# Splitting the first fetch of a block's tail values by segment, and moving three quarters of it to another queue

## The chip, the cores and the metric

The kernel runs on one core of a Trainium2 chip. The metric is the device time of one execution in microseconds (us), from three runs: the median is 1030.23 us, the lowest 1029.62 and the highest 1031.26. One further execution was recorded by the hardware profiler; all views quoted below come from that one.

The engines are named as in the profile: PE (TensorE matmuls), PEld (its weight loads), DVE (VectorE), ACT (ScalarE), POOL (GpSimd) and SP (SyncE, which here only issues transfers). A name with a q behind it (SPq, ACTq) is the engine's instruction queue when it issues a transfer. Transfers issued by SP and by ACT run on the same 16 DMA engines.

## What is computed

The program has two halves, each behind a layer norm with a residual: a recurrent attention with memory tokens (A), and a dense layer with a squared ReLU (B). Only A touches the change.

```python
for s in range(64):                     # 64 segments of 32 tokens
    xs = LN(x)[:, 32*s:32*s+32, :]      # [1, 32, 640]
    h = concat([mem, xs])               # 8 memory tokens + 32 tokens = 40
    q, k, v = h@Wq, h@Wk, h@Wv          # 32 heads of 128
    p = softmax(mask(q k^T / sqrt(128)))
    o = (p v) @ Wo                      # [1, 40, 640]
    mem = o[:, :8]                      # goes into the next segment
    out_A[32*s:32*s+32] = o[:, 8:]
h1 = x + out_A
out = h1 + (relu(LN(h1)@w1 + b1)**2) @ w2 + b2
```

The 64 segments are a chain: the memory of one is an input of the next. A query sees all memory and the tokens up to its own place; a memory query sees all 40 keys.

## The kernel before

**Blocks and steps.** Four segments make a block of 128 tokens; there are 16 blocks and 64 calls of `step(b, sp)`, block `b`, segment `sp`. Each step projects 32 rows: the 8 memory rows of this segment and its first 24 tokens. The last 8 tokens of each segment, its tail, cannot be among them, and since they do not depend on the memory they are projected ahead, for a whole block at a time (4 x 8 = 32 rows): `tail_units(b, "q" | "k" | "v")`. Queries and keys of the tails stay in SBUF. The values of the tails (`"v"`) need another layout, with the token on the partition axis within each of four groups of heads; they are written to DRAM (`vt_d`, line 279 in `tail_out`) and read back in that layout by `tails_v_in` (lines 331 to 336), four DMAs, one for each group of heads, into the tile `vt4` [128, 4 segments, 2, 128]. One such DMA moves 64 KB: 32 partitions, each 4 segments x 2 x 128 values of bf16, 2 KB that are contiguous in DRAM.

**Who reads it.** In step `sp` the four matmuls of line 452 (for each half of the heads) multiply the memory queries' weights by `vt4[r, sp, n, :]`, and one step later line 358 does the same for the tokens' queries. So a step reads only its own segment of the tile.

**The start.** Before the 64 steps, `start()` runs while the weights arrive. SP issues, in this order: rows of x, the five chunks of Wv (1 MB each, lines 117 to 120), one more piece of x, the five chunks of Wq, the five chunks of Wk, and Wo in six pieces (`load_wo`, lines 142 to 146; two of 1280 KB, four of 640 KB), then the x rows of blocks 1 and 2 (`load_x`). PE consumes the chunks as they land: `stream("v")`, `stream("q")` and `stream("k")` project block 0's first segment and its tails chunk by chunk, with the tail values of blocks 1 to 4 in between as filling. Block 0's tail values are stored by ACT's queue (line 282), and are fetched back by ACT's queue too: `tails_v_in(0, nc.scalar)` stands at line 709, behind `stream("q")`. Then comes step 0, which needs Wo at its end: `wo_rounds(main, pw, ...)`, lines 531 to 537. The order of Wo's pieces is that in which step 0 reads them; the last 14 of its 64 matmuls read the sixth piece.

**Order and waits.** The kernel is recorded under a manual schedule: each engine runs its instructions in the order in which the code calls them. Waits are added by the tile framework, which tracks the parts of tiles that an instruction reads and writes. Each DMA of the two queues takes the next of eight completion semaphores in turn, in program order, and a DMA that reuses a semaphore first waits until the DMA eight places before it has landed. So at most eight are in flight, and a queue can stand at a DMA that waits for one of the other queue. In the kernel as built, pieces 2, 4, 5 and 6 of Wo wait for the four DMAs of `tails_v_in(0)`.

**What stands behind on SP.** After the x rows of block 2, SP's next DMAs store tail values: three of blocks 5 and 6, whose rows are evacuated during step 0 into a ring of four `row` buffers (`rowtile`, line 217), then eight that had been parked elsewhere, then the four DMAs of `tails_v_in(1)`. Those three stores free `row` buffers that ACT's evacuations of step 1 write again (lines 224, 222 and 403).

Of the kernel before, what the change touches and what calls it, by code (L numbers as in the profile page):

```python
# [12 lines left out]
BF16 = mybir.dt.bfloat16  # L13
# [3 lines left out]
def kernel(  # L17
# [16 lines left out]
    nc = tc.nc  # L34
    _, S, D = A_x.shape
    _, H, E = A_Wq.shape
# [31 lines left out]
    s1 = ctx.enter_context(tc.tile_pool(name="s1", bufs=1))  # L68
    s2 = ctx.enter_context(tc.tile_pool(name="s2", bufs=2))
# [66 lines left out]
    for ch in range(2):  # L136
        nc.scalar.dma_start(out=o0[32 * ch:32 * ch + M, :].rearrange("m (c f) -> m c f", f=64),
                            in_=A_mem0[0].rearrange("m (c t f) -> t m c f", t=2, f=64)[ch])
# [25 lines left out]
    def ln_stats(b):  # L164
        xns[b] = stats(xts[b][:])

    def ln_norm(b):
        mv, rs = xns[b]
        xn = s1.tile([128, D], BF16, tag="xn", name="xn")
        xt = xts.pop(b)  # L170
        nc.vector.tensor_scalar(out=xn[:], in0=xt[:], scalar1=mv[:, 0:1], scalar2=rs[:, 0:1],
                                op0=ALU.subtract, op1=ALU.mult)
        xns[b] = xn

    def ln_transpose(b):

        xn = xns.pop(b)
        pt = mm.tile([128, 1024], BF16, tag="mm", name="pt")
        for c in range(DC):
            nc.tensor.transpose(out=pt[:, c * 128:(c + 1) * 128], in_=xn[:, c * 128:(c + 1) * 128], identity=ident[:])  # L180

        def out():
            if isinstance(b, tuple):
                hTt = s2.tile([128, DC, 4, TL, 4], BF16, tag="hTt", name="hTt")
                for c0, c1 in ((0, 2), (2, DC)):
                    nc.scalar.copy(out=hTt[:, c0:c1].rearrange("p c b k s -> p (c b) s k"),
                                   in_=pt[:, c0 * 128:c1 * 128].rearrange("p (a s k) -> p a s k", s=4, k=TL))
                hTts[b[1]] = hTt
                return
            hT4 = s2.tile([128, DC, 4, SEG], BF16, tag="hT4", name="hT4")  # L190
            ptv = pt[:, 0:640].rearrange("p (c s t) -> p c s t", c=DC, s=4)
            nc.scalar.copy(out=hT4[:, :, :, M:SEG], in_=ptv[:, :, :, 0:HD])
            hT4s[b] = hT4
        return out

    def proj(w, by, lhs, n, ps, c0, c1):

        if by == "columns":
            wr = w[:].rearrange("p (c g j n k e) -> p c n k g j e", c=DC, g=G, n=2, j=4, k=4)
        elif by == "half":  # L200
            wr = w[:].rearrange("p (c k j n e) -> p c n k j e", c=DC, k=G, n=2, j=4)
        else:
            wr = w[:].rearrange("p (c k n f) -> p c n k f", c=DC, k=G, n=2)
        for c in range(c0, c1):
            for k in range(4):
                nc.tensor.matmul(ps[32 * k:32 * k + 32, :], lhsT=lhs(c), rhs=wr[:, c, n, k], start=(c == 0), stop=(c == DC - 1))  # L206
# [10 lines left out]
    def rowtile():  # L217
        return s2.tile([128, 512], BF16, tag="row", name="row", bufs=4)

    def evac_row(which, row, ps):  # L220
        if which == "q":
            nc.scalar.mul(out=row, in_=ps, mul=scale)  # L222
        else:
            nc.scalar.copy(out=row, in_=ps)  # L224

    def flip(row, dst, n):
        nc.vector.transpose(out=dst[:, n * 16:(n + 1) * 16, 0:32], in_=row.rearrange("p (h e) -> p h e", e=32))  # L227
# [23 lines left out]
    def run(q, n):  # L251
        while n > 0 and q:
            q.pop(0)()
            n -= 1

    def tail_rows(b, c):
        return hTts[b // 4][:, c, b % 4].rearrange("p k s -> p (k s)")

    def tail_units(b, which):
        w = {"q": wq, "k": wk, "v": wv}[which]  # L260
        lhs = lambda c: tail_rows(b, c)
        st = {}

        def unit(n, c):
            def f():
                if c == 0:
                    st[n] = mmtile()
                proj(w, "columns" if which != "v" else "order", lhs, n, st[n], c, c + 1)
                if c == DC - 1:
                    tail_out(b, which, n, st[n][:])  # L270
            return f
        return [unit(n, c) for n in range(2) for c in range(DC)]

    def tail_out(b, which, n, ps):
        row = parked.pop(0) if which == "v" and 0 < b and parked else rowtile()[:]
        evac_row(which, row, ps)
        if which == "v":
            def store(eng=nc.sync):
                eng.dma_start(out=vt_d[b, 2 * n:2 * n + 2].rearrange("j r f -> r j f"),
                              in_=row.rearrange("r (j f) -> r j f", j=2))  # L280
            if b == 0:
                store(nc.scalar)
            elif b < 5:
                stores.append(store)
            else:
                store()
            return
        if n == 0:
            tails.setdefault(b, {})[which] = s2.tile([128, H, 32], BF16, tag=which + "Tt", name=which + "Tt")
        dst = tails[b][which]  # L290
        late.append(lambda: flip(row, dst, n))
# [28 lines left out]
    def tails_in(b, sp, which="qk", h0=0, h1=H):  # L320
        q, k = [tails[b][w][:].rearrange("p h (k s) -> p h s k", s=4)[:, h0:h1, sp, :] if w in which else None for w in "qk"]
        if "q" in which:
            nc.gpsimd.tensor_copy(out=qT[:, h0:h1, SEG:NK], in_=q)
        if "k" in which:
            nc.gpsimd.tensor_copy(out=kT[:, h0:h1, SEG:2 * SEG].rearrange("p h (j k) -> p h j k", k=TL),  # L325
                                  in_=k.unsqueeze(2).to_broadcast([128, h1 - h0, 4, TL]))

    vt4s, stores = {}, []
    vt_d = dram.tile([NB, 4, 128, 2 * E], BF16)

    def tails_v_in(b, eng):

        vt4s[b] = s2.tile([128, 4, 2, E], BF16, tag="vt4", name="vt4")
        src = vt_d[b].rearrange("j (g k s) f -> g j k (s f)", g=G, s=4)
        for g in range(G):
            eng.dma_start(out=vt4s[b][32 * g:32 * g + 32].rearrange("p s u e -> p (s u e)"), in_=src[g])

    def store_main(o, s):
        for ch in range(2):
# [38 lines left out]
    def step(b, sp, v=None):  # L378
# [8 lines left out]
        if sp == 1 and b + 1 < NB:  # L387
            tails_v_in(b + 1, nc.sync)
# [278 lines left out]
    def start():  # L667

        v = s2.tile([128, EG], BF16, tag="v", name="v")
        main = lambda c: hT4s[0][:, c, 0, :]  # L670
        units = []

        def stream(which, w, dst):
            pa = pop.tile([128, 4, 512], F32, tag="po", name="pa")
            for c in range(DC):
                for n in range(2):
                    proj(w, "half" if which == "v" else "columns", main, n, pa[:, n, :], c, c + 1)
                for n in range(2):
                    proj(w, "order" if which == "v" else "columns", lambda c: tail_rows(0, c), n, pa[:, 2 + n, :], c, c + 1)
                if c < DC - 1:  # L680
                    run(units, DC)
            for n in range(2):
                if which == "v":
                    nc.scalar.copy(out=v[:, n * 512:(n + 1) * 512], in_=pa[:, n, :])
                else:
                    row = rowtile()[:]
                    evac_row(which, row, pa[:, n, :])
                    flip(row, dst, n)
                    tail_out(0, which, n, pa[:, 2 + n, :])
                    run(late, 100)  # L690
                    tails_in(0, 0, which, n * 16, (n + 1) * 16)
            if which == "v":
                for n in range(2):
                    tail_out(0, which, n, pa[:, 2 + n, :])

        stream("v", wv, None)
        ln_stats(("t", 1))
        ln_norm(("t", 1))
        units += tail_units(1, "v")
        run(units, DC)  # L700
        ln_transpose(("t", 1))()
        run(units, DC)
        units += tail_units(2, "v") + tail_units(3, "v")
        stream("q", wq, qT)
        for n in range(2):
            spread(n)
        units += tail_units(4, "v")
        run(units, 2 * DC)
        tails_v_in(0, nc.scalar)
        units += tail_units(1, "q")  # L710
        stream("k", wk, kT)
        units += tail_units(1, "k")
        run(units, 2 * DC)
        run(late, 100)
        return v
# [11 lines left out]
    load_x(1)  # L727
    ln_transpose(("t", 0))()
    v0 = start()
    halves = [h for b in range(8, NB) for h in (tail_units(b, "v")[:DC], tail_units(b, "v")[DC:])]  # L730
    for b in range(NB):
        for sp in range(4):
# [40 lines left out]
            e = b * 4 + sp - (NS - 7)  # L773
# [30 lines left out]
    for t in range(S // NT):  # L804
# [32 lines left out]
        for q in range(NK4):  # L837
# [18 lines left out]
            for hh in range(2):  # L856
                b = t * NK4 + pr + 2 * hh
# [38 lines left out]
```

## Time and profile before

| | us |
|---|---|
| median of three runs | 1030.23 (1029.62 to 1031.26) |
| profiled execution, its own time | 1033.91 |
| its span, first to last instruction | 1031.8 |
| PE busy | 975.2 (95%) |
| DVE / ACT / POOL busy | 617.2 / 533.7 / 309.9 |
| mean granted TensorE clock | 0.993 |
| Wo's last piece lets PE go on (step 0) | 62.51 |
| PE begins step 1 | 65.49 |

PE is busy almost without a break from step 1 to the end; the start, up to some 65 us, is another stage, in which PE waits for weights. All places of the change lie in this stage or right behind it.

Rows of the timeline and of the chain give the start in us from the first instruction, the duration in us, and what ran; "x20" is the number of instructions merged into a row, and a bracket tells how long the engine had been idle before and what ended it. Rows of the window view give, for a stretch of time, each engine's busy time with its number of instructions, the granted TensorE clock (1.00 is full), the mean busy share of the 16 DMA engines and the bytes that they moved in GB/s. The view of DMA queues gives packets, megabytes and the share of 16 engines' time; q1 is SP's ring, q10 is ACT's, q8 and q14 carry instructions.

### The profile page before, as it was taken

To read this page: it belongs to the slowest core of one execution; us is meant where nothing else is said; L and a number is where in the kernel's file an instruction comes from. 1 tells how busy PE (TensorE), PEld (TensorE's weight loads), DVE (VectorE), ACT (ScalarE), POOL (GpSimd) and SP (SyncE) were. 2 spreads that over 40 slices of the span, in tenths; PEclk is the share of its full clock that TensorE was granted. 3 is DMA by queue.
4 is the path that set the end of the run, shared out by engine and by line. 5 is a ranking of instruction groups with operands and counts; after the bars stand their busy time and mean duration, and the time that the engine had idled before them with its cause. 6 is when DMAs were issued, how large, how long until landed. Compare 5 with 4: busy or idle time off the path is not lost.

```text
span 1031.8 us, 58965 instructions
## 1 busy us (share of the span) xinstructions
PE 975.2 (95%) x26960; PEld 578.7 (56%) x26960; DVE 617.2 (60%) x1740; ACT 533.7 (52%) x1229; POOL 309.9 (30%) x803
## 2 busy tenths in 40 slices
PE   6779899999999999999999999999999999999998
PEld 2345455655655555556655665555566565555565
DVE  2256566766666666666766666666665576566432
ACT  3335555555555555555555555555555555534431
POOL 1023333333333333333333232323333333343210
PEclk9989999999999999999999999999999999999999
DMA  9960101000101010000000000000000110612200
GB/s 361 381 195 21 23 7 31 7 25 6 35 7 29 7 37 12 23 14 25 16 21 16 15 27 14 22 14 27 15 21 9 47 34 7 195 59 68 77 26 26
DMA packets 38968, 51.57 MB, mean 50 GB/s; under 512 B 5952, under 2 KB 34752, under 8 KB 36800
## 3 DMA queue, kind: packets, MB, share of 16 engines
q1 hardware_dynamic: 37936, 47.29, 14.0%
q8 instruction: 210, 3.44, 1.4%
q10 hardware_dynamic: 784, 0.53, 0.2%
q14 instruction: 38, 0.31, 0.1%
HBM read 38.37 MB, written 9.44 MB: 46 GB/s over the span
## 4 chain that ended last, share of the span: by engine, by line
PE 88%; DMA 5%; issue 2%; DVE 2%; ACT 1%; SPq 1%; ACTq 0%; DVEq 0%; POOL 0%
PE ps L206 48%; PE pw L238 15%; PE y L847 6%; PE ps L815 5%; PE ps L238 3%; PE po L447 2%; PE po L353 2%; PE sm L419 2%; DMA vt_d<-row 1%; PE ps L491 1%; DMA wv<-in_A_Wv_dram 1%; DMA wo<-in_A_Wo_dram 1%; PE pm L316 1%; DMA vt<-vt_d 1%; DMA wq<-in_B_w_dram 1%
## 5 line engine op out<-in xcount | busy, mean ns | idle before, releaser
L206 PEld LDWEIGHTS <-hT 128*32 128x32 bf16 x7680 | 196.8, 97 | 179.9 <-issue 19.3
L238 PE MATMUL pw<-wo,oT 128*32 128x320 bf16 x4224 | 186.6, 301 | 9.3 <-issue 6.0
L206 PE MATMUL ps<-wv,hT 128*32 128x512 bf16 x2520 | 171.6, 379 | 2.6 <-issue 2.0
L206 PE MATMUL ps<-wq,hT 128*32 128x512 bf16 x2520 | 159.6, 381 | 5.3 <-DVE hT L318 5.3
L206 PE MATMUL ps<-wk,hT 128*32 128x512 bf16 x2520 | 159.2, 381 | 0.1
L238 PEld LDWEIGHTS <-oT 128*32 128x32 bf16 x4224 | 106.8, 96 | 62.3 <-issue 15.5
L222 ACT ACTIVATE row<-ps 128x512 bf16<-128x512 f32 x156 | 93.3, 599 | 74.8 <-PE ps L206 74.8
L227 DVE STREAM_TRANSPOSE qT<-row 128x512 bf16<-128x512 bf16 x128 | 90.3, 705 | 65.5 <-ACT row L222 65.4
L546 POOL TENSOR_TENSOR pkt<-ek,rk 128x64 bf16<-128x64 bf16 x64 | 19.0, 296 | 363.6 <-DVE rk L544 363.6
L224 ACT CAST row<-ps 128x512 bf16<-128x512 f32 x115 | 68.0, 591 | 32.9 <-PE ps L206 32.7
L325 POOL COPY kT<-kTt 128x1024 bf16<-128x1024 bf16 (+1 forms) x65 | 71.9, 1106 | 13.0 <-DVE kTt L227 13.0
L372 POOL COPY qz<-qT 128x96 bf16<-128x96 bf16 x126 | 33.6, 267 | 138.1 <-DVE qT L227 137.9
L206 PEld LDWEIGHTS <-hTt 128*32 128x32 bf16 x1920 | 54.1, 98 | 33.7 <-issue 4.5
L245 ACT COPY otmp<-pw 64x320 f32<-64x320 f32 x66 | 27.9, 422 | 83.2 <-PE pw L238 83.2
L246 DVE TENSOR_TENSOR o<-pw,otmp 64x320 bf16<-64x320 f32 x66 | 31.8, 482 | 63.2 <-ACT otmp L245 63.2
L363 ACT CAST oT<-po 128x512 bf16<-128x512 f32 x128 | 68.7, 589 | 1.6
L521 ACT CAST v<-ps 128x512 bf16<-128x512 f32 x63 | 36.9, 586 | 59.6 <-PE ps L206 59.6
L227 DVE STREAM_TRANSPOSE kT<-row 128x512 bf16<-128x512 bf16 x65 | 46.1, 709 | 32.1 <-ACT row L224 32.1
L542 DVE TENSOR_REDUCE zk<-ek 128x8 f32<-128x320 bf16 x64 | 31.1, 486 | 53.8 <-ACT ek L540 53.8
L847 PE MATMUL y<-wq,wk 128*128 128x320 bf16 x416 | 61.0, 299 | 0.2 <-DVE wk L824 0.2
L403 ACT CAST row<-ps 128x256 bf16<-128x256 f32 x126 | 40.8, 375 | 31.0 <-PE ps L206 29.9
L500 ACT CAST v<-ps 128x512 bf16<-128x512 f32 x63 | 36.9, 586 | 30.0 <-PE ps L206 30.0
(113 smaller groups left out, 1633.5 us busy)
## 6 DMA issues: line engine op xcount, KB each, us to landing
wv<-in_A_Wv_dram SPq DMA_DIRECT2D x5, 1024.0 KB
wq<-in_A_Wq_dram SPq DMA_DIRECT2D x5, 1024.0 KB
wk<-in_A_Wk_dram SPq DMA_DIRECT2D x5, 1024.0 KB
vt<-vt_d SPq DMA_DIRECT2D x60, 64.0 KB
xt<-in_A_x_dram SPq DMA_DIRECT2D x20, 160.0 KB
vt_d<-row SPq DMA_DIRECT2D x22, 128.0 KB
wo<-in_A_Wo_dram SPq DMA_DIRECT2D x2, 1280.0 KB
wo<-in_A_Wo_dram SPq DMA_DIRECT2D x4, 640.0 KB
```

What stands on the lines that cost most here:

```text
L206: nc.tensor.matmul(ps[32 * k:32 * k + 32, :], lhsT=lhs(c), rhs=wr[:, c, n, k], start=(c == 0), stop=(c == DC - 1))
L222: nc.scalar.mul(out=row, in_=ps, mul=scale)
L224: nc.scalar.copy(out=row, in_=ps)
L227: nc.vector.transpose(out=dst[:, n * 16:(n + 1) * 16, 0:32], in_=row.rearrange("p (h e) -> p h e", e=32))
L238: nc.tensor.matmul(pw[32 * j:32 * j + 32, 0:DH], lhsT=lhs(p), rhs=wov2[:, head(p), ch], start=(h == 0), stop=(h == 15))
L325: nc.gpsimd.tensor_copy(out=kT[:, h0:h1, SEG:2 * SEG].rearrange("p h (j k) -> p h j k", k=TL), in_=k.unsqueeze(2).to_broadcast([128, h1 - ...
L363: nc.scalar.copy(out=oTg[:, n, :, :, M:NK], in_=po[:, :, n * 128:(n + 1) * 128].rearrange("p g (j q) -> p g j q", q=32))
L403: nc.scalar.copy(out=row[:, u * 256:(u + 1) * 256], in_=ps[:, u * 256:(u + 1) * 256])
L500: nc.scalar.copy(out=v[:, 0:512], in_=ps0[:])
L521: nc.scalar.copy(out=v[:, 512:1024], in_=ps1[:])
L815: nc.tensor.matmul(ps[:], lhsT=w1[:, c, fc * 128:(fc + 1) * 128], rhs=hnT[:, c, :], start=(c == 0), stop=(c == DC - 1))
L847: nc.tensor.matmul(y[:, hh, 0:DH], lhsT=f1T[:, fc, k * 128:(k + 1) * 128], rhs=w2[:, fc, cs], start=(fc == 0), stop=False, skip_group_chec ...
```

## The change

`tails_v_in` gets two more arguments, the first segment and the one behind the last, and fetches only these; the tile is made at the first call for a block. Its only caller with a part is `start()`: ACT's queue fetches segment 0 of block 0 (four DMAs, each 32 packets of 512 B in place of 2 KB), and SP's queue fetches segments 1 to 3 (four DMAs, each 32 packets of 1536 B). All other blocks are fetched as before.

```diff
-    def tails_v_in(b, eng):
+    def tails_v_in(b, eng, s0=0, s1=4):
 
-        vt4s[b] = s2.tile([128, 4, 2, E], BF16, tag="vt4", name="vt4")
+        if b not in vt4s:
+            vt4s[b] = s2.tile([128, 4, 2, E], BF16, tag="vt4", name="vt4")
         src = vt_d[b].rearrange("j (g k s) f -> g j k (s f)", g=G, s=4)
+        f0, f1 = s0 * 2 * E, s1 * 2 * E
         for g in range(G):
-            eng.dma_start(out=vt4s[b][32 * g:32 * g + 32].rearrange("p s u e -> p (s u e)"), in_=src[g])
+            eng.dma_start(out=vt4s[b][32 * g:32 * g + 32].rearrange("p s u e -> p (s u e)")[:, f0:f1], in_=src[g, :, :, f0:f1])
...
         units += tail_units(4, "v")
         run(units, 2 * DC)
-        tails_v_in(0, nc.scalar)
+        tails_v_in(0, nc.scalar, 0, 1)
+        tails_v_in(0, nc.sync, 1, 4)
         units += tail_units(1, "q")
```

On SP the four new DMAs stand behind Wo's six pieces and the x rows of block 1, and ahead of the x rows of block 2 and the stores. On no engine does another instruction move. In the program as built, step 0's matmuls of line 452 wait for ACT's four DMAs alone, and those of step 1 wait for SP's four. Since four DMAs are added to the turn of the eight semaphores, each of the eight next DMAs waits for another predecessor than before: the x rows of block 2 wait for Wo's fourth piece, the three stores of step 0's rows for Wo's fifth and sixth piece and for the x rows of block 1.

## The prediction

> **What bounds the kernel now.** I read the page first (PE is busy 95% of the span, so only a place where PE stands still can give time), then the chain that ended last, then PE's and ACT's timelines from 40 to 90 us, and last the DMA views. The chain and PE's timeline around the end of step 0:
>
> ```profile
> span 1031.8 us, 58965 instructions
> PE 975.2 (95%) x26960; PEld 578.7 (56%) x26960; DVE 617.2 (60%) x1740; ACT 533.7 (52%) x1229; POOL 309.9 (30%) x803
> ...
> 36.33 7.68 DMA vt<-vt_d
> ...
> 51.27 11.21 DMA wo<-in_A_Wo_dram
> ...
> 43.03 0.61 PE L206 MATMUL pa<-wk,hT 128*32 128x512 bf16 x8 [1.13 <-DMA wk<-in_A_Wk_dram]
> 46.06 1.04 PE L206 MATMUL pa<-wk,hT 128*32 128x512 bf16 x8 [1.98 <-DMA wk<-in_A_Wk_dram]
> ...
> 58.78 0.57 PE L238 MATMUL pw<-wo,oT 128*32 128x320 bf16 x10
> 60.79 0.46 PE L238 MATMUL pw<-wo,oT 128*32 128x320 bf16 x8 [1.44 <-issue]
> 62.51 1.25 PE L238 MATMUL pw<-wo,oT 128*32 128x320 bf16 x14 [1.27 <-DMA wo<-in_A_Wo_dram]
> ...
> 65.49 2.32 PE L206 MATMUL ps<-wq,hT 128*32 128x512 bf16 x20 [0.34 <-DVE hT L318]
> ```
>
> The chain holds the fetch of the tail values (36.33 to 44.03) and then Wo: PE could not go on before 62.51, when Wo's last piece had landed. From there to the start of step 1 at 65.49 there is only a chain of short operations. So what the change is worth is how much earlier Wo is complete, as far as PE is ready by then. Behind 65.49 PE is the bound; a shift there is carried to the end.
>
> The queues, in four stretches: 40 to 49 us, 20 to 30, 49 to 58 and 63 to 65:
>
> ```profile
> DMA packets 1433, 2.92 MB, mean 325 GB/s; under 512 B 57, under 2 KB 1151, under 8 KB 1279
> q1 hardware_dynamic: 1289, 2.66, 94.4%
> q10 hardware_dynamic: 144, 0.26, 9.5%
> ...
> DMA packets 833, 4.16 MB, mean 416 GB/s; under 512 B 66, under 2 KB 344, under 8 KB 344
> ...
> DMA packets 2598, 3.26 MB, mean 362 GB/s; under 512 B 63, under 2 KB 2597, under 8 KB 2597
> q1 hardware_dynamic: 2597, 3.24, 106.8%
> q8 instruction: 1, 0.02, 0.8%
> ...
> q1 hardware_dynamic: 709, 0.35, 59.8%
> ```
>
> The rings are full throughout. With Wk's 8 KB packets they move 416 GB/s, with Wo's 1280 B packets 362, but only 325 while ACT's 0.26 MB fetch passes.
>
> **The fetch on ACT's queue, the gain.** In 40 to 49 the fetch holds 9.5% of 16 engines for 9 us, 13.7 engine-us, 95 ns for each of 144 packets (128 of them its own). SP's ring got 154 packets of 8 KB (1433 less 1279; 1.26 MB, 3.0 us at 416 GB/s) and 1.40 MB of Wo (3.9 us at 362) through: 6.9 us of work in 9.0. So the fetch costs the weights 2.1 us on average over the engines, more than its 13.7 / 16 = 0.86 us.
>
> The change keeps 128 packets there but of 512 B. No row has such a read. The nearest are the 512 B stores of 63 to 65 (59.8% of 32 engine-us over 709 packets: 27 ns) and Wo's 1280 B reads of 49 to 58 (106.8% of 144 engine-us over 2597: 59 ns). The slope from 1280 to 2048 B (59 to 95 ns) leads to 23 ns at 512 B, so I take 27: 3.5 engine-us in place of 13.7. If the loss goes with the engine time, 0.5 us of 2.1 stay: 1.6 us gained. With 59 ns it is 0.9; if the loss goes with the number of packets, nothing.
>
> The average isn't all, since each piece of Wo needs its slowest DMA engine. A fetch of the same shape with empty rings (issued 118.89):
>
> ```profile
> 118.89 2.69 SPq L336 DMA_DIRECT2D vt<-vt_d  x4
> ...
> 121.00:122.00 1.00, 1.00 (x24) 0.54 (x20) 0.71 (x1) 0.51 (x2) 0.57 (x3) 1.00 0.22 59
> 122.00:123.00 1.00, 1.00 (x44) 0.57 (x36) 0.70 (x2) 0.52 (x2) 0.00 (x0) 1.00 0.24 86
> ...
> 58.00:59.00 1.00, 1.00 (x28) 0.53 (x23) 0.00 (x0) 0.00 (x0) 0.00 (x0) 1.00 1.08 359
> ...
> 62.00:63.00 1.00, 0.49 (x9) 0.31 (x11) 0.00 (x0) 0.00 (x0) 1.00 (x2) 0.73 0.74 224
> ```
>
> The last two columns are the share of the 16 engines and GB/s. The fetch never holds more than 0.24 of them, 3.8 engines, though nothing else wants them. So the 13.7 engine-us lie on about four engines, 3.4 us each, 1.3 more than the mean loss of 2.1; that fits the rate falling from 359 to 224 GB/s while Wo ends, some engines being done and others not. After the change the four carry 0.9 us, some 0.3 over the mean. Of the 1.0 us between I count half, because others then come last: an engine that carries one instruction packet (q8: 0.8% of 144 engine-us, 1.15 us) is late by that. Wo complete: 1.6 + 0.5 = 2.1 us earlier, at 60.4; bounds 0 and 2.6.
>
> The Trainium skill, "DMA: Bandwidth & Descriptors", section "Why a DMA increments its semaphore by 16 and not by 1", gives a rule for this: a transfer runs on the largest number up to 16 that divides the outermost sizes of both sides. Here these are 32 partitions and 4 pieces of `vt_d`, so four engines; by that rule, the trace agrees (0.24 of 16). Were the fetch spread over 16 engines, the sum for Wo would be 1.6 us without the 0.5.
>
> **Is PE ready by then?** At 60.79 PE comes from 1.44 us of "issue", and its eight matmuls end at 61.25. If that stayed, the gain would end at 62.51 - 61.25 = 1.3 us. But PE's work in step 0 hangs on Wk's last piece (46.06), and that too lies behind fetch packets: the last two pieces are 3.03 us apart (43.03 to 46.06) where 1.05 MB at 416 GB/s take 2.5, so two pieces are late by 1.0 in all; three quarters of that is 0.7. PE's eight then end at 60.55, and the last 14 matmuls begin there: 1.9 us earlier rather than 2.1.
>
> **PE's clock.** The same view and PE's timeline further on:
>
> ```profile
> 66.00:67.00 1.00, 1.00 (x16) 0.36 (x12) 0.89 (x3) 0.00 (x0) 0.10 (x1) 0.50 0.80 228
> ...
> 69.52 1.25 PE L206 MATMUL ps<-wq,hT 128*32 128x512 bf16 x20
> ...
> 76.77 1.26 PE L238 MATMUL pw<-wo,oT 128*32 128x320 bf16 x32
> ...
> 79.93 1.25 PE L206 MATMUL ps<-wq,hT 128*32 128x512 bf16 x20
> ...
> 82.08 1.25 PE L206 MATMUL ps<-wq,hT 128*32 128x512 bf16 x20
> ```
>
> The granted clock is 0.50 behind the waits. Step 1's first two projections take 65.49 to 69.52, 4.0 us, where step 2's take 79.93 to 82.08, 2.15: 1.9 us lost. The 14 matmuls take 1.25 where 32 take 1.26 at full clock: 0.7 more. With the stretch of little work (58.78 to 65.49) 1.9 us shorter, between nothing and all of this 2.6 may go; or the half clock lasts to the same instant and covers more work, 1.9 us of it, which would cost at most half, 1.0, less the 0.7. I take -0.3.
>
> **SP's queue.** Four issues are added:
>
> ```profile
> 53.09 2.55 SPq L126 DMA_DIRECT2D xt<-in_A_x_dram  x2
> 55.73 4.30 SPq L279 DMA_DIRECT2D vt_d<-row  x3
> ...
> 66.34 2.75 SPq L336 DMA_DIRECT2D vt<-vt_d  x4
> ...
> 80.71 0.84 DVE L153 BATCH_NORM_STATS2 lnst<-xt 128x6 f32<-128x320 bf16 x2
> ...
> 69.75 0.59 ACT L224 CAST row<-ps 128x512 bf16<-128x512 f32 x1 [1.28 <-PE ps L206]
> 70.83 0.60 ACT L222 ACTIVATE row<-ps 128x512 bf16<-128x512 f32 x1 [0.49 <-PE ps L206]
> 71.91 0.65 ACT L403 CAST row<-ps 128x256 bf16<-128x256 f32 x2 [0.48 <-PE ps L206]
> ...
> 74.33 0.20 PE L452 MATMUL po<-pTm,vt 32*128 32x32 bf16 x4
> ```
>
> Each takes 2.75 / 4 = 0.7 us of SP, which waits for transfers anyway. Their 0.19 MB stands behind Wo in the same ring, so it takes nothing from Wo; on four engines 32 packets each at about 70 ns (between 59 and 95) are 2.2 us, landed by about 60.4 + 0.5 (x rows) + 2.2 = 63.1, for matmuls at 74.33. The x rows of block 2 come 2 to 3 us later, for DVE at 80.71. The three stores were issued from 55.73 on; now they wait for Wo's fifth and sixth piece and for x rows, so they go out from about 59.5 to 61 and land, behind the fetch and 0.4 MB of their own (1.1 us at 362), at 65 to 66. ACT writes their rows again at 69.75, 70.83 and 71.91, less 2: some 2 to 4 us of slack, price zero. `tails_v_in(1)` moves from 66.34 by 1 to 2 us, for step 4 past 110. ACT's own queue issues four DMAs as before.
>
> **The sum.** -1.9 (Wo, capped by PE) - 0.3 (clock) = -2.2 us: the profiled execution's 1033.91 would be 1031.7. It stands 3.7 above the median of the runs; taken off 1030.23 it gives 1028.0.
>
> **The rivals.**
> - *PE or other DMA engines hold it back.* The 1.44 us of "issue" are no wait that the profile names; if they end where they ended, or engines with instruction packets set Wo's end, the gain is 0.3 to 1.3: 1029.4.
> - *Packets cost by number.* The fetch keeps its 128 packets, and the weights lose the 2.1 us as before: 1030.2, no gain. Against it: 95 ns at 2048 B and 59 at 1280 go with the size.
> - *The clock comes back too.* If the shorter wait spares PE the half clock, up to 2.6 us more go; with two thirds of it, 1026.3. For it: the half clock begins only at about 62.5, so late that 1.9 us matter. Against: activity from 59 to 62.5 stays low. The Trainium skill, "TensorE: Matmul & The Clock Gate", section "Part 1: The HAM clock gate (the "warmup" mystery)", has the clock set by activity in free-running windows of 3.4 us; the profiled stretch at 0.50 fits, and by it this term would change from run to run.
> - *Slower: the stores.* They stand behind the new fetch on SP. If they land after 71.91 - 2 = 70, each us beyond it holds ACT's evacuation, and with it scores and PE in step 1, 1:1. At 75 it costs 5 less the 2: 1033. That needs them to land 9 us later than worked out.
>
> **How the numbers follow.** Forecast 0.52 (gain 1.4 to 3.0, 1027.2 to 1028.8), held back 0.20, clock 0.14, packets by number 0.07, stores 0.07. The bound of 0.2% is 2.06 us, about what a measurement of this kernel can tell from no change; of the forecast's range some two thirds lie beyond it: faster 0.34 + 0.14, about 0.49; same 0.18 + 0.20 + 0.07, about 0.44; slower 0.07. The range from 1025.9 to 1030.1 leaves out the stores, half of "by number" and the end of the clock's case.
>
> **What would show it.** Right: Wk's last piece lets PE go on at about 45.4 and Wo's last at 60.3 to 60.6; the rate of 40 to 49 us is well above 325 GB/s, with q10 at a quarter of its megabytes and under 4% of the engines; step 1 begins at about 63.5. ACT's rows of step 1 wait for PE, not for `vt_d`. Wrong: q10's share stays near 9%, or a wait for `vt_d<-row` stands before ACT in step 1, or the "issue" before PE's eight matmuls grows by what Wo gained, or the half clock covers more of step 1.

## The result and the profile after

The changed kernel takes 1026.38 us, median of 11 runs (1023.83 to 1029.10), against 1030.23 for the kernel before (11 runs, 1027.79 to 1031.26): a ratio of 0.9968, 95% interval 0.9956 to 0.9979, so 2.2 to 4.5 us less, 3.3 by the ratio. The forecast was 2.2 us less.

Single executions of one kernel lie 5.3 us apart here and up to 8.5 in the later series. Both profiled ones are slower than their medians, the one before by more: 1027.67 us, 1.3 above its median, against 1033.91, 3.7 above. So the two traces are compared at single places, the times only as groups of runs. One execution each of two kernels further below (1236.67 and 1050.96 us, mean clock 0.75 and 0.95) is left out of the ratios.

The chain of waits after the change, its two rows of interest, and PE's timeline around the end of step 0:

```profile
span 1025.5 us, 58960 instructions
...
35.59 6.96 DMA vt<-vt_d
...
48.54 10.66 DMA wo<-in_A_Wo_dram
```

```profile
44.90 0.62 PE L206 MATMUL pa<-wk,hT 128*32 128x512 bf16 x8 [1.70 <-DMA wk<-in_A_Wk_dram]
...
58.59 0.46 PE L238 MATMUL pw<-wo,oT 128*32 128x320 bf16 x8 [1.25 <-issue]
59.24 0.72 PE L238 MATMUL pw<-wo,oT 128*32 128x320 bf16 x14 [0.20 <-DMA wo<-in_A_Wo_dram]
61.05 0.30 PE L316 MATMUL pm<-ident,o 128*32 128x8 bf16 x20 [1.08 <-DVE o L246]
61.69 2.32 PE L206 MATMUL ps<-wq,hT 128*32 128x512 bf16 x20 [0.34 <-DVE hT L318]
63.80 2.35 PE L206 MATMUL ps<-wk,hT 128*32 128x512 bf16 x20
```

The same rows as before, earlier: Wk's last piece lets PE go on at 44.90 in place of 46.06, Wo's last at 59.24 in place of 62.51, and step 1 begins at 61.69 in place of 65.49. Part of this is chance. ACT reads out the last row that waits for a store, ahead of the fetch, in both kernels; before, then after:

```profile
36.32 0.60 ACT L222 ACTIVATE row<-pa 128x512 bf16<-128x512 f32 x1 [1.27 <-DMA vt_d<-row]
```

```profile
35.59 0.60 ACT L222 ACTIVATE row<-pa 128x512 bf16<-128x512 f32 x1 [0.89 <-DMA vt_d<-row]
```

0.73 us lie between them before anything that was changed has run, which would leave 2.5 of Wo's 3.27. What the transfers did is in the view of the DMA queues, from 40 to 49 us as before:

```profile
DMA packets 2002, 3.36 MB, mean 373 GB/s; under 512 B 57, under 2 KB 1864, under 8 KB 1864
q1 hardware_dynamic: 1866, 3.28, 102.0%
q10 hardware_dynamic: 135, 0.06, 2.5%
```

373 GB/s in place of 325; ACT's ring holds 2.5% of the engines in place of 9.5%: 3.6 engine-us, 27 ns a packet. 138 packets of 8 KB (2002 less 1864; 1.13 MB, 2.7 us at 416 GB/s) and 2.15 MB of Wo (5.9 us at 362) make 8.66 us of work in 9.0, so the weights lose 0.3 us there, where they lost 2.1.

Behind the waits, two rows of the window view, with the clock in the column ahead of the share of the DMA engines, and ACT's timeline in step 1:

```profile
61.00:62.00 1.00, 0.62 (x24) 0.35 (x28) 0.57 (x3) 0.00 (x0) 0.27 (x2) 0.50 0.21 56
...
67.00:68.00 1.00, 1.00 (x20) 0.41 (x16) 0.53 (x1) 0.13 (x1) 0.00 (x0) 0.90 0.15 11
```

```profile
66.20 0.58 ACT L224 CAST row<-ps 128x512 bf16<-128x512 f32 x1 [1.54 <-DMA vt_d<-ht]
```

This execution fell to half clock behind the waits all the same, two us earlier than before. But the kernel before was at half clock once more, right behind Wk's last piece, where the changed one ran at full clock; a row of the window view, before and then after, and the first matmuls of step 0 that read the keys, again before and then after:

```profile
46.00:47.00 1.00, 0.94 (x12) 0.44 (x15) 0.00 (x0) 0.00 (x0) 0.00 (x0) 0.50 1.07 273
```

```profile
46.00:47.00 1.00, 1.00 (x24) 0.58 (x20) 0.39 (x1) 1.00 (x2) 0.00 (x0) 1.00 1.07 358
```

```profile
51.86 0.30 PE L419 MATMUL sm<-kT,qz 128*32 128x64 bf16 x16 [1.24 <-POOL kT L325]
```

```profile
49.84 0.30 PE L421 MATMUL sm<-kT,qz 128*32 128x64 bf16 x16 [1.72 <-POOL kT L325]
```

From Wk's last piece (46.06 and 44.90) to these matmuls it is 5.80 us before and 4.94 after, 0.86 less. One pair of profiles doesn't show what the clock gave on average. ACT's first row of step 1 is put down to a store of tail values; but PE's projection, started at 63.80 and 2.35 long, had ended only at 66.15, so the store cost 0.05 us at most.

### The profile page after: what moved, and what is told of

It reads as the page before. It is cut to its first block, busy times and chain, and to the rows that moved or that the text cites. A ratio compares the mean times of both kernels' runs of the same rounds, so it can differ in the third digit from the quotient of the medians.

```text
span 1025.5 us, 58960 instructions
## 1 busy us (share of the span) xinstructions
PE 971.4 (95%) x26951; PEld 576.6 (56%) x26960; DVE 619.0 (60%) x1740; ACT 533.2 (52%) x1229; POOL 309.1 (30%) x803
## 4 chain that ended last, share of the span: by engine, by line
PE 87%; DMA 6%; DVE 2%; issue 2%; ACT 1%; SPq 1%; ACTq 0%; DVEq 0%; POOL 0%; POOLq 0%
PE ps L206 48%; PE pw L238 15%; PE y L850 5%; PE ps L818 4%; PE ps L238 3%; PE po L449 2%; PE po L355 2%; PE sm L421 2%; DMA wq<-in_B_w_dram 1%; DMA vt_d<-row 1%; PE ps L493 1%; DMA wv<-in_A_Wv_dram 1%; DMA wo<-in_A_Wo_dram 1%; PE pm L316 1%; DMA vt<-vt_d 1%
```

## The experiments

My theory: ACT's fetch delays Wo by its time on about four DMA engines; with a quarter of it left, other engines come last; and the clock adds a little. Rivals: the fetch costs by the number of its packets; it costs only its bytes spread over all engines; most of the gain is the clock, not the transfer. Ratios are to the kernel before on the same chip; they are not exactly those of the medians, and where the two differ I go by the ratio. A time difference "by the ratio" between two kernels is the difference of their ratios; each ratio is uncertain by 1.0 to 2.0 us. "Half clock" is (1 - mean granted clock) x span / 0.5, averaged over the timed runs: how long PE ran at half clock in one execution. Beside the first four kernels, the kernel before took 1032.25 us (35 runs) with 10.1 us of half clock.

**The change, again.** No edit.

> The changed kernel as it is, beside the kernels below on one chip. Theory A (the four DMA engines that carry ACT's fetch set the end of Wo, and most of the gain is Wo's end): the median stays 2.5 to 4.5 us under that of the kernel before, near 1026.4; Wo's last 14 matmuls start about 3 us before those of the kernel before (59.24 against 62.51 in the profiles). Rival B (part of the 3.85 us was chance, since PE's clock and its short unnamed stalls differ from run to run): nearer to 2.2 us.

1028.26 us, 0.9964 (0.9949 to 0.9979), half clock 4.1 us. PE's timeline:

```profile
59.66 0.72 PE L238 MATMUL pw<-wo,oT 128*32 128x320 bf16 x14 [0.22 <-DMA wo<-in_A_Wo_dram]
61.47 0.29 PE L316 MATMUL pm<-ident,o 128*32 128x8 bf16 x20 [1.08 <-DVE o L246]
62.09 1.26 PE L206 MATMUL ps<-wq,hT 128*32 128x512 bf16 x20 [0.34 <-DVE hT L318]
```

and ACT's, where the row of step 1 now waits for PE:

```profile
64.49 0.59 ACT L224 CAST row<-ps 128x512 bf16<-128x512 f32 x1 [0.48 <-PE ps L206]
```

This execution never left full clock (20 projections in 1.26, not 2.32), and SP's queue delays nothing in step 1.

**Half of the fetch in place of a quarter.** ACT fetches segments 0 and 1.

```diff
-        tails_v_in(0, nc.scalar, 0, 1)
-        tails_v_in(0, nc.sync, 1, 4)
+        tails_v_in(0, nc.scalar, 0, 2)
+        tails_v_in(0, nc.sync, 2, 4)
```

> Segments 0 and 1 on ACT's queue (packets of 1024 B), 2 and 3 on SP's: one size changed. Theory A: the four engines carry 32 packets of about 47 ns each, 1.5 us, in place of 0.9 (a quarter, 27 ns) and 3.4 (all, 105 ns in that stretch); Wo's end and the time come 0.6 us after those of the changed kernel, about 1027.0. Rival C (other engines come last once the four are relieved): the whole gain stays, 1026.4. Rival D (the loss goes by bytes: half of them, two thirds of what the change moved): 2/3 of the gain, 1027.7.

1029.60 us, 0.9974 (0.9960 to 0.9989), half clock 7.0 us. PE's timeline, then the queues from 40 to 49 us:

```profile
60.45 0.72 PE L238 MATMUL pw<-wo,oT 128*32 128x320 bf16 x14 [1.21 <-DMA wo<-in_A_Wo_dram]
```

```profile
DMA packets 1833, 3.21 MB, mean 356 GB/s; under 512 B 60, under 2 KB 1693, under 8 KB 1693
q10 hardware_dynamic: 141, 0.13, 4.8%
```

The same number of packets at twice the size: 4.8% of the engines, 356 GB/s, Wo 0.8 us later than in the run above. The engines' time goes with the bytes (a quarter, a half, all: 2.5, 4.8, 9.5%), not with the number, and so does Wo's end (59.66, 60.45, 62.51). In the times the run lies 1.0 us above the one before it, between theory A (0.6) and rival D (1.2 to 1.3), which these intervals can't tell apart.

**Three quarters of the fetch between Wo's pieces.** SP's fetch goes ahead of Wo's last two pieces.

```diff
-    def load_wo():
+    def load_wo(k0, k1):
...
-        for h0, k in ((0, 8), (16, 8), (1, 4), (17, 4), (9, 4), (25, 4)):
+        for h0, k in ((0, 8), (16, 8), (1, 4), (17, 4), (9, 4), (25, 4))[k0:k1]:
...
         tails_v_in(0, nc.sync, 1, 4)
+        load_wo(4, 6)
+        load_x(1)
...
-    load_wo()
-    load_x(1)
+    load_wo(0, 4)
```

> As the changed kernel, but SP's fetch of segments 1 to 3 stands ahead of the last two pieces of Wo (and of the x rows of block 1) in SP's queue. The same transfers, another place. Theory A: the four engines carry 32 packets of 1536 B at 69 ns more ahead of Wo's end, 2.2 us: the last matmuls of step 0 start about 2.2 us later than in the changed kernel, 61.4, and the time is 1028.0 to 1028.6. Rival E (the transfer is spread over all engines): 0.2 MB at 362 GB/s, 0.5 us, 1026.9. Rival F (the order doesn't matter, since PE's own chain is the bound): 1026.4.

1033.38 us, 1.0006 (0.9991 to 1.0021), half clock 10.1 us: the whole gain is gone. PE's timeline:

```profile
61.93 1.25 PE L238 MATMUL pw<-wo,oT 128*32 128x320 bf16 x14 [1.45 <-DMA wo<-in_A_Wo_dram]
64.26 0.30 PE L316 MATMUL pm<-ident,o 128*32 128x8 bf16 x20 [1.08 <-DVE o L246]
64.90 2.32 PE L206 MATMUL ps<-wq,hT 128*32 128x512 bf16 x20 [0.34 <-DVE hT L318]
```

Wo comes 2.3 us later than in the first run (61.93 against 59.66). 0.2 MB spread over all engines would be 0.5 us at 362 GB/s; that rival falls. The time went up by more than theory A said: 4.3 us by the ratio against the run "again". Wo's 2.3 and 6 us more of half clock, at the price found below (0.26 us each, 1.6), make 3.9 of it. The window view and the queues from 54 to 57 us:

```profile
53.00:54.00 1.00, 0.97 (x36) 0.36 (x28) 0.03 (x1) 0.57 (x3) 0.00 (x0) 1.00 1.07 360
...
55.00:56.00 1.00, 1.00 (x44) 0.59 (x40) 0.84 (x2) 0.27 (x1) 0.00 (x0) 1.00 1.08 260
56.00:57.00 1.00, 1.00 (x26) 0.52 (x20) 0.00 (x0) 0.00 (x0) 0.00 (x0) 1.00 1.16 273
```

```profile
DMA packets 687, 0.89 MB, mean 295 GB/s; under 512 B 33, under 2 KB 686, under 8 KB 686
q1 hardware_dynamic: 686, 0.87, 108.4%
```

While the fetch passes, the rate falls from 360 to 260 GB/s at a full share of the engines.

**No fetch on ACT's queue.** The first segment's tail values are left out: zeros stand in their place, so the output lacks their part.

```diff
-        tails_v_in(0, nc.scalar, 0, 1)
+        vt4s[0] = s2.tile([128, 4, 2, E], BF16, tag="vt4", name="vt4")
+        nc.gpsimd.memset(vt4s[0][:, 0], 0.0)
         tails_v_in(0, nc.sync, 1, 4)
```

> As the changed kernel, but nothing is fetched on ACT's queue: segment 0 of block 0's tail values is left out and filled with zeros by POOL, so segment 0's outputs lack these values. It prices what the quarter still costs. Theory A: the four engines lose their last 0.9 us, but other engines then come last (the changed kernel's profile has the rate fall from 365 to 198 GB/s between 56 and 60 us), so 0 to 0.9 us, about 1026.0. Rival G (the loss goes with the number of packets, which the change kept): most of the 2.1 us that the fetch cost is still there and goes now, 1024.3.

1029.49 us, 0.9977 (0.9962 to 0.9992), half clock 5.0 us. The queues from 40 to 49 us and PE's timeline:

```profile
DMA packets 1899, 3.42 MB, mean 380 GB/s; under 512 B 48, under 2 KB 1748, under 8 KB 1748
```

```profile
59.73 1.12 PE L238 MATMUL pw<-wo,oT 128*32 128x320 bf16 x14 [0.60 <-DMA wo<-in_A_Wo_dram]
```

With the last quarter away too, Wo comes no earlier (59.73 against 59.66; three profiles of the change spread from 59.24 to 60.01), and the time is not shorter either. So the quarter no longer sets Wo's end; nothing that shows is left to be had from this fetch. That also refutes a cost by packets: the change would then have gained nothing and this kernel all.

**PE kept busy, in the kernel before.** Idle matmuls, whose product nobody reads, stand where PE waits: six ahead of Wk's last chunk, six among Wo's last rounds, four ahead of the memory rows. They are meant to take no wait away, only the low activity. Line numbers rise by five. The kernel before took 1032.49 us beside this and the next three kernels (23 runs, half clock 10.6 us).

```diff
+    def idle_mm(n):
+        d = mmtile()
+        for _ in range(n):
+            nc.tensor.matmul(d[:], lhsT=ident[:], rhs=wq[:, 0:512], start=True, stop=True)
...
-        wo_rounds(main, pw, 8, 16)
+        if ready:
+            wo_rounds(main, pw, 8, 12)
+            idle_mm(6)
+            wo_rounds(main, pw, 12, 16)
+        else:
+            wo_rounds(main, pw, 8, 16)
...
+            if ready:
+                idle_mm(4)
...
+                if which == "k" and c == DC - 1:
+                    idle_mm(6)
```

> The kernel before, with 16 matmuls of 128 x 512 added whose results nobody reads, where PE waits: six ahead of Wk's last piece, six ahead of the part of step 0 that waits for Wo's last two pieces, four while the memory rows are made from it. One suspected cost taken away: PE's half clock, without moving any transfer. Theory K (of the gain of some 4 us, Wo's earlier end is about 2.5 and the rest is PE's clock, which halves less often since PE waits less): 1.0 to 1.7 us faster than the kernel before, at a mean granted clock of 0.9975 or more where the kernel before has 0.995; Wo's last matmuls start no earlier. Rival L (the rest of the gain has nothing to do with the clock): within 0.5 us of the kernel before, whatever the clock.

1030.10 us, 0.9978 (0.9968 to 0.9988), half clock 1.9 us. PE's timeline:

```profile
62.36 0.72 PE L243 MATMUL pw<-wo,oT 128*32 128x320 bf16 x14 [0.49 <-DMA wo<-in_A_Wo_dram]
64.17 0.29 PE L321 MATMUL pm<-ident,o 128*32 128x8 bf16 x20
64.80 1.26 PE L206 MATMUL ps<-wq,hT 128*32 128x512 bf16 x20 [0.34 <-DVE hT L323]
```

Wo comes when it came before (62.36, 62.51), and still 2.3 us are gained (1.2 to 3.3): no transfer was moved, so I put it down to the clock, 0.26 us for each us of half clock less.

**PE kept busy, in the changed kernel.** The same without the six among Wo's rounds:

```diff
             wo_rounds(main, pw, 8, 12)
-            idle_mm(6)
             wo_rounds(main, pw, 12, 16)
```

> The changed kernel, with ten such matmuls: six ahead of Wk's last piece and four while the memory rows are made (it has no wait of over 0.3 us for Wo's last pieces to fill). Theory K: its clock has less left to lose, 0.3 to 1.0 us faster than the changed kernel, and 2.0 to 3.0 us faster than the kernel before with its 16 matmuls: the part of the change that is Wo's end alone. Rival L: no difference to the changed kernel, and 4 us to the kernel before with its matmuls.

0.9947 (0.9933 to 0.9962; only 4 runs), 1027.0 us by the ratio, half clock 1.0 us. PE's timeline:

```profile
59.90 0.72 PE L243 MATMUL pw<-wo,oT 128*32 128x320 bf16 x14 [0.67 <-DMA wo<-in_A_Wo_dram]
61.70 0.29 PE L321 MATMUL pm<-ident,o 128*32 128x8 bf16 x20
62.33 1.26 PE L206 MATMUL ps<-wq,hT 128*32 128x512 bf16 x20 [0.34 <-DVE hT L323]
```

With the clock nearly out of both, the pair before and after differs by 2.46 us at Wo's end (62.36 to 59.90), 2.47 at step 1 (64.80 to 62.33), and 0.0031 in the ratio, 3.2 us. This is the transfer's part, by one pair of profiles and by two ratios whose difference is uncertain by some 1.8 us. It is the best ratio to the kernel before of all that ran; the changed kernel wasn't run beside it.

**The same between Wo's pieces.** The fetch between Wo's pieces, with all 16 idle matmuls; both edits stand above. Beside this kernel and the last two of this section the kernel before took 1031.79 us (26 runs, half clock 10.2).

> The kernel with SP's fetch ahead of Wo's last two pieces, with the 16 idle matmuls that the kernel before was given. Theory M (that order costs 2.3 us through Wo's end, 61.93 against 59.66, and the rest of its 5 us against the changed kernel is PE's half clock): Wo's last matmuls stay near 62, the clock goes to 0.998 or more, and the time falls by about 2.5 us, to about the level of the kernel before with its idle matmuls (2.4 us under the kernel before). Rival N (the rest is something else, such as the later stores and instruction packets): it stays at the kernel before or above.

1030.63 us (11 runs), 0.9979 (0.9964 to 0.9995), half clock 1.3 us.

```profile
62.57 1.25 PE L243 MATMUL pw<-wo,oT 128*32 128x320 bf16 x14 [1.39 <-DMA wo<-in_A_Wo_dram]
```

Wo as late as before the change, and the time that of the kernel before with idle matmuls (0.9978). Wk's last piece comes at 45.19 here, as after the change, so its earlier end alone gives nothing. So of the change only Wo's end and the clock show; the other moves (SP's four issues, stores, completion semaphores) are worth nothing that can be seen within the intervals.

**Real work as filling.** The second half of block 6's tail values, which step 1 projected, goes into step 0; once in the changed kernel, once in the kernel before.

```diff
-                fill += tail_units(5, "v") + tail_units(6, "v")[:DC]
+                fill += tail_units(5, "v") + tail_units(6, "v")
...
-                fill += tail_units(6, "v")[DC:] + tail_units(7, "v")[:DC]
+                fill += tail_units(7, "v")[:DC]
```

> The changed kernel, with the second half of block 6's tail values (20 matmuls) moved from step 1's filling to step 0's, where it runs while the memory rows are made. The wait there is 1.1 us (59.96 to 61.05) and the 20 matmuls take 1.08 to 1.25: about 1.1 us of PE's work leaves step 1, so 1.1 us faster than the changed kernel, and under Theory K 0.3 to 1.0 more through the clock: 1.4 to 2.1 in all. Against it: at half clock the 20 take twice as long and hold up the memory rows by 1 us, and the ring of four row buffers gets one more user, whose store stands behind SP's fetch; then no gain.

> The kernel before with the same filling moved. 1.1 us of PE's work into a wait, so 1.1 to 2.1 us faster than the kernel before. The difference between the two kernels with this filling is the change once more, measured a second time: 2.5 (Wo's end) to 4 us (with all of the clock).

After: 1027.2 us by the ratio, 0.9949 (0.9933 to 0.9965), half clock 3.4 us. Before: 1032.47 us, 1.0000 (0.9987 to 1.0014), half clock 6.4 us. PE's timeline of the latter:

```profile
62.46 1.25 PE L238 MATMUL pw<-wo,oT 128*32 128x320 bf16 x14 [1.44 <-DMA wo<-in_A_Wo_dram]
65.38 0.59 PE L316 MATMUL pm<-ident,o 128*32 128x8 bf16 x20
66.34 1.90 PE L206 MATMUL ps<-wq,hT 128*32 128x512 bf16 x16 [0.37 <-DVE hT L318]
```

In the kernel before, half clock has begun when the filling runs (1.25 for 14 matmuls), and step 1 begins at 66.34, 0.85 later than without, which can have eaten what was saved (one profile). The price of half clock doesn't hold here either: 4.2 us less of it would be 1.1 us, and nothing was gained (to within 1.4). Why it gave something after the change (0.9949 against 0.9964, 0.9968 and 0.9969 without it, with overlapping intervals) stays open, and so does why the two kernels with this filling lie 5.3 us apart by the ratio where 2.5 to 4 were expected.

**Filling and six idle matmuls ahead of Wk's last chunk,** in the changed kernel: the filling's edit and, of the idle matmuls', only the first place.

> The changed kernel with the six idle matmuls ahead of Wk's last piece and with the second half of block 6's tail values in the wait behind Wo's end, in place of the four idle ones. Theory K: both waits are filled, so a clock near 1.0 (about 1.5 us under the changed kernel, as the ten idle matmuls gave), and up to 1.1 us of work out of step 1 besides: 1.5 to 2.6 us under the changed kernel, 5.5 to 6.5 under the kernel before. Against it: the same filling gave the kernel before nothing, as one more store waits and step 1 has less to fill its own waits with; then as with the ten idle matmuls, 5.0 to 5.5 under the kernel before.

1028.27 us, 0.9956 (0.9937 to 0.9975), half clock 0.5 us: 4.5 us under the kernel before, where 5.0 to 6.5 were expected; no better than either alone.

**The change, a third time.**

> The changed kernel once more, beside the two others: 0.9966 of the kernel before, 3.5 us (between 2.2 and 4.5 by the two comparisons so far), at a granted clock between 0.997 and 0.998.

1029.00 us, 0.9969 (0.9955 to 0.9982), half clock 3.4 us; Wo's last piece:

```profile
60.01 0.72 PE L238 MATMUL pw<-wo,oT 128*32 128x320 bf16 x14 [0.72 <-DMA wo<-in_A_Wo_dram]
```

Three measurements of the change: 0.9968, 0.9964, 0.9969, so 3.2 to 3.7 us.

## Why the prediction was right and where it was wrong

The direction, the range and the main mechanism (the fetch delays Wo) held (1026.38 in 1025.9 to 1030.1). The gain was 3.3 us in place of 2.2, above the 1.4 to 3.0 that I gave the forecast itself, and the median lies on the rival in which the clock comes back too (1026.3). So the terms need looking at.

- **The loss to the fetch: right in size, its cause left open.** 0.3 us of 2.1 stay, predicted 0.5; 27 ns for a packet, as taken from the stores. Two readings were loose and cost the sum nothing that shows: the 95 ns are a mean with 16 packets of a few bytes, while the 128 of 2 KB took 105; and the 8 KB packets of 20 to 30 us are mostly Wq's, of the same size as Wk's. The prediction didn't say why the loss is 2.1 and not the 0.86 of the fetch's own time. The trace keeps the time of every packet, and these settle it: from 40 to 49 us 1094 packets of Wo took 75 ns in place of 60 (50 to 58 us), 154 of Wk 348 in place of 315 (36 to 40), together 21 engine-us, 1.3 us on each of 16; with 0.86 that is 2.2. So most of the loss is that the other packets become slower while `vt_d` is read. In the changed kernel they took 61 and 316.
- **Four engines: right in kind, mis-sized.** "Of the 1.0 us between I count half" was too little. Over the profiles whose last 14 matmuls wait for Wo, the three with the old order (before, and before with idle matmuls or filling) have it at 62.51, 62.36 and 62.46, the four with the new order (the change three times, and with idle matmuls) at 59.24, 59.66, 60.01 and 59.90: 62.44 against 59.70, 2.7 us, forecast 2.1. Of that 1.8 is the mean loss (2.1 less 0.3), which leaves 0.9 for the unevenness, nearly all of the 1.0. That other engines come last is consistent with the kernel after, where taking the last quarter away gave nothing. No view names the engines, so that the four came last before is argued, not shown.
- **"Is PE ready by then?": wrong.** I let PE's "issue" idle move only as much as Wk's last piece and capped the gain at 1.9. PE's eight matmuls began 2.2 us earlier (60.79 to 58.59), and PE waited for Wo in every profile of the change and in the one with idle matmuls (0.20 to 0.72). The rows split the 2.2. Wk's last piece gives 1.16, of which 0.73 is chance; over the same seven profiles it is 0.7 (45.80 to 45.09), as predicted. "Issue" gives 0.2 (1.44 to 1.25); its cause isn't shown. The stretch behind Wk's last piece gives 0.86, and that is what the step left out: before, PE ran it at half clock. The prediction shows the row (1.04 us for eight matmuls of Wk, 0.62 at full clock) and put no time to it. At full clock the stretch took 4.94 or 4.95 us in the profiles of both orders.
  So the rival "held back" fell for the change as profiled. But with the filling in the changed kernel the half clock fell behind Wk's last piece again (1.04 us for the eight), the last 22 matmuls of Wo began together at 60.20 behind "issue", and PE didn't wait for the last piece: in such an execution PE does hold the gain back.
- **The clock: right in sign, perhaps too small.** -0.3 was worked out from one execution at half clock. Over the runs the kernel before spends 10.1 to 10.6 us at half clock, the changed one 5.4, 4.1 and 3.4: 6 us less on average, at 0.26 us each 1.5. But the gain of 3.2 to 3.7 less the transfer's 2.5 (Wo in the pair with idle matmuls) to 3.2 (its times) leaves only 0 to 1.2. Within that the runs don't split it; the intervals reach 1.0 to 1.8 us to each side. The price itself is uncertain (1.2 to 3.3 us for 8.7), and the kernel before with the filling didn't bear it out. So the rival's number was met more by the transfer than by its own mechanism.
- **The skill's windows.** The Trainium skill, "TensorE: Matmul & The Clock Gate", section "Part 1: The HAM clock gate (the "warmup" mystery)", has the clock set in windows that run freely; that the same kernel fell to half clock in one profile (61.69, 2.32 us for 20 projections) and not in another (62.09, 1.26) agrees with it.
- **SP's queue: right, zero.** ACT's row of step 1 waits for PE (64.49 above), and with Wo late again the time is that of the kernel before, not above it, though the four issues are still there. The rival "stores" fell.
- **Packets by number: fell,** by the halved fetch and by the one left out.

The rest of the 6.3 us between the two profiled spans, some 2.5 us behind the start of step 1, isn't explained; the medians do not show it.

## What to carry to other kernels

A small transfer can delay what stands behind it by far more than its bytes: 0.2 MB ahead of Wo's last pieces cost 2.3 us in place of 0.5, partly because Wo's own packets became slower meanwhile, and the rest probably because its packets lie on about four DMA engines; 0.06 MB in small packets cost nothing that shows. Fetch only what the next step reads while weights stream, and the rest behind them. A wait near the start can be worth more than its length when PE's clock falls behind it; price that over many runs, since one profile shows one draw, and try idle matmuls in the waits (0.9978 here, with nothing else changed).

## What the runs showed of the hardware

- Matmuls that nobody reads, put into three waits of the first 65 us, take the kernel before from 10.6 to 1.9 us of half clock and make it 2.3 us faster (1.2 to 3.3) of 1032.
- While `vt_d` is read, the 16 engines move 260 GB/s at a full share, where Wo alone moves 360; a packet took 76 ns on average (108.4% of 48 engine-us over 686), against 59. The three-quarter fetch, 0.2 MB, lasts some 2.5 us at that rate; 0.65 MB pass in this time, 0.45 of them Wo's, which alone take 1.2 us. The other 1.3 us are lost on average, more than the 0.5 of its bytes. The times of single packets in this trace tell how: from 55 to 57 us 298 of Wo's packets took 89 ns on average, 98% of them over 70 ns, where 850 from 50 to 53 us took 60 and 1% over 70. A fetch on about four of 16 engines can't stand ahead of nearly all of Wo's packets, so the packets on the other engines became slower too; by what, no run here shows. In the kernel before, from 46 to 48 us, it is the same with 2 KB reads (81 ns, 92% over 70); beside the 512 B reads of the changed kernel, from 44 to 46 us, hardly (62 ns, 7%). A layout of `vt_d` whose read lies on all engines wasn't tried.
